# Preparing the keys of units 4 to 7 beside the first block inverse, and one list of VectorE background work

## The chip, the cores and the metric

The kernel runs on one core of one Trainium2 chip. Its metric is the device time of one execution in microseconds (us). The kernel before was timed three times: 815.86, 823.84 and 824.90 us, so the median is 823.84 us and the runs lie 1.1% apart.

## The reference

The work is a delta-rule linear attention (4 batches, 8 heads, 768 steps, head width 48), and then one dense block with a sigmoid-gated activation on the joined heads:

```python
k_n = k / (np.linalg.norm(k, axis=-1, keepdims=True) + 1e-06)
state = np.zeros((B, H, D, D))                    # B, H, S, D = 4, 8, 768, 48
for t in range(S):
    y[:, :, t] = einsum('bhd,bhde->bhe', q[:, :, t], state)
    v_old = einsum('bhde,bhd->bhe', state, k_n[:, :, t])
    state += beta[:, :, t, None, None] * einsum('bhd,bhe->bhde', k_n[:, :, t], v[:, :, t] - v_old)
x = y.transpose(0, 2, 1, 3).reshape(3072, 384)
h = x @ w_in                                      # w_in 384 x 2048
out = (h / (1 + exp(-1.702 * h))) @ w_out         # w_out 2048 x 384
```

The two weight matrices arrive as 64-bit floats. The kernel turns each pair of 32-bit words of a weight into one 32-bit float itself; q, k, v and beta are used as 32-bit floats.

## The kernel before, in words

**Units.** The sequence is cut into 6 chunks of 128 steps; with 4 batches that makes 24 units, numbered chunk by chunk (units 0 to 3 are chunk 0 of the four batches, units 4 to 7 chunk 1). For each unit the keys are normalised (`normalize...`), turned to `kT` on TensorE (`turn`, tile psT), and their Gram matrix `G` is formed (`gram`, tile psG). The recurrence inside a unit becomes a triangular solve in four blocks of 32 rows. The inverses of all 32x32 diagonal blocks of four units (later of two) are formed together on VectorE by `invert`, in the tiles NT (input, then result) and YB: one multiply by beta, 15 steps over the two 16x16 diagonal halves (`P<-NT,YB` and a reduce into YB), a copy on ScalarE of one half into NT (`NT<-YB 128x256`, called X1 below), then ten larger products that use this copy, and a last multiply by beta into NT (called the end of the inverse). The result goes through DRAM (Yd) into the tiles XB.

**Solving.** `hops(a, b)` solves two units side by side in eight hops. In each hop TensorE multiplies by the inverse (psU), ScalarE copies the result into US, TensorE forms what it takes from the lower blocks (psR), and VectorE subtracts that from V. `put_out` then forms the unit's outputs and state (psY) and writes them, transposed, into xT. `scores` turns the queries (psT, QS) and forms the masked scores (psQ, M).

**The dense block.** `hidden` multiplies xT of two units with w_in (tile ph) and applies the activation on ScalarE into gT; it is written as a generator of 16 slices of TensorE work. `both_written` and `written` multiply gT with w_out (tile po) for the first four units; from the third pair on, `seven` does it with seven half-size products instead of eight, for which `combined` has to form four sums and differences of w_out blocks on GpSimd (POOL), once.

**Order.** All queues are written by hand: nearly every instruction is pinned to program order on its engine, and a recording helper puts them all on one line of the source (L109 in the profile). The start runs: normalise and turn units 0 to 3; send the 32x32 diagonal blocks of their Gram matrices (psD, tile `TW`) through DRAM (Nd) into NT; `gram` 0 to 3; scores of units 0 to 3, with the first inverse beside them on VectorE; hops of units 0 and 1; hops of units 2 and 3 with the first slices of `hidden` between them; then the keys of units 4 to 7 (`keys`, `prepare`: normalise, turn, gram, `G` through DRAM into NT); the second inverse beside the rest of `hidden`; then the loop `woven` over units 3 to 24, which fills the solves with slices of the dense block from a queue.

**Weights.** `conversions` yields after each VectorE instruction, and `fill(n)` emits the next n of them. One piece of a weight takes five: mask the exponent (`ts`, followed by an activation on ScalarE), set the mantissa bits into a scratch in TW (`ts`), add the low word (`stt`), merge the sign (`stt`), multiply (`stt`). The raw words of w_in are kept in the w_out tile, two quarters at a time; finishing piece 1 and piece 3 of w_in issues the fetch of the next quarter on the SP queue.

**Padding work.** `warm(n)` issues n matmuls whose results are not used.

Of the kernel before, what the change touches and what calls it, by code (L numbers as in the profile page):

```python
# [18 lines left out]
def kernel(  # L19
# [179 lines left out]
    turns = [0]  # L199

    def conversion(dst, raw, shape):

        lo, hi = raw[:, :, :, 0], raw[:, :, :, 1]
        ts, stt = vec.tensor_scalar, vec.scalar_tensor_tensor
        AND, OR = ALU.bitwise_and, ALU.bitwise_or
        E1 = 1 << 20  # L210
        p = dst.bitcast(I32)
        ts(p, hi, 0x7FF * E1, None, op0=AND)
        act.activation(p, p, ACT.Relu, scale=8.0, bias=low)
        yield
        turns[0] ^= 1
        at = 3072 + turns[0] * 768
        t = TW[:, at : at + shape[0] * shape[1]].bitcast(I32).rearrange("p (j n) -> p j n", j=shape[0])
        f = t.bitcast(F32)
        ts(t, hi, E1 - 1, E1, op0=AND, op1=OR)
        yield  # L220
        stt(out=f, in0=lo.bitcast(U32), scalar=2.0**-32, in1=t, op0=ALU.mult, op1=ALU.add)
        yield
        stt(out=p, in0=hi, scalar=-(1 << 31), in1=p, op0=AND, op1=OR)
        yield
        stt(out=dst, in0=f, scalar=2.0**-20, in1=dst, op0=ALU.mult, op1=ALU.mult)
        yield
# [60 lines left out]
    converting = conversions()  # L287

    def fill(n):
        for _ in range(n):  # L290
            next(converting, None)

    ready = {}
    inverse = {}

# [53 lines left out]

    def transposed(src, dst):  # L350
        psT = ps_big.tile([128, NP, 128], F32, tag="big", name="psT")
        flat = src.rearrange("p h d -> p (h d)")
        for j in range(NP):
            pe.transpose(psT[:, j, :], flat[:, j * 128 : (j + 1) * 128], ident)
        act.activation(dst, psT, ACT.Copy)
# [24 lines left out]
    def turn(n):  # L380
        kTs[n] = wk.tile([128, NP, 128], F32, tag="kT", name="kT", bufs=5)
        transposed(KN[n % len(KN)], kTs[n])
# [28 lines left out]
    def diagonal(b, D_):  # L411

        kT = kTs[b]
        ps = [ps_seq.tile([128, NP, 128], F32, tag="seq", name="psD") for _ in range(2)]
        for h in range(H):
            r = slice(h % 2 * 64, h % 2 * 64 + D)
            pe.matmul(
                ps[h % 2][:, h // 2], lhsT=kT[r, h // 2, :], rhs=kT[r, h // 2, :],
                start=True, stop=True,
            )  # L420
        for e in range(2):
            for blk in range(NB):
                u = slice(blk * BS, (blk + 1) * BS)
                copy = vec.tensor_copy if e == 0 or blk == 0 else act.copy
                copy(D_[u, e::2, :], ps[e][u, :, u])
# [91 lines left out]
    class Step:  # L517
# [114 lines left out]
        def state(self, psS=None):  # L632
# [3 lines left out]
            for h in range(H):  # L636
# [4 lines left out]
                )  # L641
            St = ST[:, self.b, 0 : NP * D].rearrange("p (j d) -> p j d", j=NP)
            vec.tensor_tensor(St, psS, St, op=ALU.add)

        def outputs(self, state=False):
# [5 lines left out]
            if state:  # L651
                self.state(self.psS)
# [67 lines left out]
    def combined():  # L720

        for o, a, b in ((T1, W12, W11), (T2, W22, T1), (T3, W22, W12), (T4, W21, T2)):
            add(o, a, b, sub_)
# [160 lines left out]
    def follow(n):  # L884
# [8 lines left out]
        if n % HB == 0 and n > B:  # L893
            h = (n - 1) // HB
            gT, sums = [], []
            queue.append(hidden(xTs[h], gT, slice(0, NTH), 1.3, sums))
# [73 lines left out]
    for i in range(B, len(KN)):  # L970
        pool.memset(KN[i][:, :, D:DP], 0.0)

# [13 lines left out]
    for b in range(B):  # L986
# [3 lines left out]
        )  # L990
    for b in range(B):
        load(b, ((QP, q),), sync)
    for b in range(B):
        load_values(b, sync)
    fetch_in(1, other_queue)
    for n in range(B, len(KN)):
        load(n, ((KN, k),), sync)
# [3 lines left out]
    for b in range(B):  # L1001
        gram(b)
        warm(NA)
    late_U = spare("U")[:, 0 : H * D + XR]
    pair = [new_step(n) for n in range(B)]
    inverting = invert(0)
    for n in range(B):
# [4 lines left out]
        if n == 0:  # L1012
            ahead_of(inverting, 18)
    run(inverting)
    pool.memset(late_U[:, H * D :], 0.0)
    for s in pair:
        s.select()
    fill(5)
# [9 lines left out]
    def put_out(s):  # L1028
        s.queries()
        s.outputs(True)  # L1030
        steps.pop(s.n)

    def keys():

        def unit(n):
            yield from normalize_mixed(n)
            yield from prepare(n)

        work = [unit(n) for n in range(B, 2 * B)]
        for t in range(18):  # L1040
            for u in range(B):
                s = t - 3 * u
                if s >= 0 and s % 2 == 0:
                    next(work[u], None)
            yield
        for w in work:
            run(w)

    path = hops(*pair[:2])
    for i in range(2 * NB):  # L1050
        together(*next(path))
        warm(NU)
        fill(1)
    for s in pair[:2]:
        put_out(s)
        fill(1)
    load(7, ((KN, k),), sync)
# [16 lines left out]
    preparing = keys()  # L1074
    for i in range(2 * NB):
        together(*next(path))
        if i > 2:
            feed()
        fill(2)
        ahead_of(preparing, 2 if i else 0)  # L1080
    for s in pair[2:]:
        put_out(s)
        feed()
        fill(2)
        ahead_of(preparing, 2)
# [4 lines left out]
    while not ("in", 7) in done:  # L1090
        fill(1)
    run(preparing)
    inverting = invert(1)
    first = new_step(B)
    for i in range(25):
        ahead_of(inverting, 1)
# [5 lines left out]
    run(inverting)  # L1102
    while ffn:
        feed()
    fill(10)
    def last_written():
        yield from written(*units[HB], gTs[1])
        combined()

    queue = [both_written(0, gTs[0]), last_written()]  # L1110
# [34 lines left out]
```

## Time and profile before

| what | value |
|---|---|
| runs | 815.86, 823.84, 824.90 us (median 823.84) |
| profiled execution | span 813.5 us from the first to the last instruction; the page gives no other time of it, and the three runs are 2.4 to 11.4 us longer than this span |
| TensorE busy | 748.9 us, 92% of the span; mean granted clock 0.943 |
| VectorE, ScalarE, GpSimd busy | 501.4, 238.5 and 249.4 us |
| weight-load side of TensorE | 636.4 us |
| DMA | 54.45 MB, mean 67 GB/s |
| chain that ended last | PE 70%, DVE 16%, DMA 4%, POOL 3% |

In the profile PE is TensorE, DVE is VectorE, ACT is ScalarE, POOL is GpSimd and SP the engine that issues most DMAs. A timeline line gives the start and the duration in us, the engine, the line, the operation, output and input tile with partitions x elements, and how many instructions were merged; in brackets stands the idle time before it and what ended that. In a table by stage each engine has its busy time and its instructions, then come the granted TensorE clock (1 is full speed) and the share of the DMA engines.

### The profile page before, as it was taken

The page shows a single profiled execution, that of the slowest core. Times are in us where ns is not written, and L with a number is a line of the kernel's source. Part 1 is how long each engine was busy: PE and PEld are TensorE (multiplying, and loading weights), DVE is VectorE, ACT ScalarE, POOL GpSimd, SP SyncE. Part 2 cuts the span into 40 slices and gives each one's busy share as a digit, 9 for nine tenths or more (in the row PEclk, how much of TensorE's full clock was granted, in tenths as well). Part 3 has the DMA queues.
Part 4 walks back from the last instruction along what each step waited for, and adds up shares of the span by engine and source line. Part 5 has one row for each costly group of instructions (what it writes and reads, how often), then busy time and mean ns, then how long its engine had stood idle before and what let it go on. Part 6 is the DMA issues. An engine that isn't in the chain of part 4 may idle for free.

```text
span 813.5 us, 19675 instructions
## 1 busy us (share of the span) xinstructions
PE 748.9 (92%) x8464; PEld 636.4 (78%) x8464; DVE 501.4 (62%) x1029; ACT 238.5 (29%) x523; POOL 249.4 (31%) x210
## 2 busy tenths in 40 slices
PE   8678889777789779999999999999999999999998
PEld 6566668644456669889888898898898898998988
DVE  5797581998578667668767777786676681110000
ACT  3332263223323322242232232332422312312120
POOL 5011030011023826235254262282160330502213
PEclk9576599889799989999999999999999999999999
DMA  9945466244112410420421323224204102000000
GB/s 163 148 74 106 102 173 163 43 111 118 55 50 66 102 45 18 103 63 18 106 53 42 83 54 74 58 56 103 56 18 94 21 15 47 2 25 2 22 3 19
DMA packets 143654, 54.45 MB, mean 67 GB/s; under 512 B 113664, under 2 KB 138368, under 8 KB 143568
## 3 DMA queue, kind: packets, MB, share of 16 engines
q1 hardware_dynamic: 141936, 48.42, 27.0%
q0 software_dynamic: 1536, 4.52, 2.3%
q8 instruction: 66, 1.08, 0.6%
q10 hardware_dynamic: 96, 0.26, 0.1%
q14 instruction: 20, 0.16, 0.1%
HBM read 33.13 MB, written 18.87 MB: 64 GB/s over the span
## 4 chain that ended last, share of the span: by engine, by line
PE 70%; DVE 16%; DMA 4%; POOL 3%; issue 3%; SPq 2%; ACT 1%; DVEq 0%; POOLq 0%
PE ph L109 25%; PE po L109 24%; PE psY L109 6%; PE psU L109 5%; DVE P L109 4%; PE psQ L109 3%; DVE YB L109 3%; PE psT L109 2%; DVE TW L109 2%; PE psG L109 2%; SPq L109 2%; PE psR L109 2%; DVE NT L109 2%; DVE w_out L109 2%; POOL TW L711 1%
## 5 line engine op out<-in xcount | busy, mean ns | idle before, releaser
L109 PE MATMUL ph<-xT,w_in 128*128 128x256 f32 x1152 | 268.7, 390 | 0.0
L109 PEld LDWEIGHTS ph<-xT,w_in 128*128 128x128 f32 x1152 | 219.8, 194 | 33.3 <-DVE V L109 1.4
L109 PE MATMUL po<-w_out,gT 128*128 128x192 f32 (+1 forms) x736 | 152.8, 361 | 18.7 <-DVE w_out L109 11.0
L109 PEld LDWEIGHTS po<-w_out,gT 128*128 128x128 f32 x736 | 122.3, 193 | 37.2 <-DVE w_out L109 14.8
L711 POOL TENSOR_TENSOR gT<-gT 128x512 f32<-128x512 f32 x80 | 105.8, 1331 | 124.6 <-ACT gT L109 114.1
L109 DVE TENSOR_TENSOR V<-V,psR 64x384 f32<-64x384 f32 (+1 forms) x96 | 53.3, 556 | 134.7 <-PE psR L109 133.5
L109 DVE TENSOR_TENSOR P<-NT,YB 64x2 f32<-64x2 f32 (+9 forms) x200 | 98.4, 492 | 6.4
L109 ACT ACTIVATE gT<-ph 128x512 f32<-128x512 f32 x92 | 54.9, 596 | 152.9 <-PE ph L109 152.8
L109 PEld LDWEIGHTS psU<-V,XB 32*32 32x32 f32 x1536 | 61.6, 109 | 31.5 <-issue 16.5
L109 DVE TENSOR_REDUCE YB<-P 64x2 f32<-64x2 f32 (+9 forms) x200 | 81.8, 409 | 6.9
L109 PE MATMUL po<-TW,gT 128*128 128x192 f32 x480 | 83.0, 328 | 0.0
L109 ACT COPY US<-psU 32x384 f32<-32x384 f32 x92 | 43.2, 469 | 125.0 <-PE psR L109 115.4
L109 PE MATMUL psU<-V,XB 32*32 32x48 f32 x1536 | 73.0, 209 | 6.5 <-DVE V L109 4.8
L109 PEld LDWEIGHTS po<-TW,gT 128*128 128x128 f32 x480 | 77.9, 190 | 1.1 <-issue 0.3
L109 PE MATMUL psR<-US,G 32*32 32x48 f32 x2208 | 63.1, 207 | 0.6 <-ACT US L109 0.5
L578 POOL TENSOR_SCALAR_AFFINE_SELECT M<-M 128x1024 f32<-128x1024 f32 x19 | 23.6, 1245 | 123.5 <-DVE M L109 62.1
L109 DVE TENSOR_TENSOR o<-o,po 128x192 f32<-128x192 f32 x40 | 13.5, 351 | 75.8 <-PE po L109 75.3
L109 PEld LDWEIGHTS psR<-US,G 32*32 32x32 f32 x2208 | 53.5, 108 | 2.0 <-ACT US L109 1.1
L94 POOL DMA_DIRECT2D KN<-in_k_dram x15 | 14.4, 959 | 99.0 <-PE psY L109 99.0
L109 DVE TENSOR_TENSOR P<-NT 64x512 f32<-64x512 f32 (+7 forms) x50 | 43.0, 860 | 2.1
L109 PE MATMUL ps_warm<-ident 128*128 128x256 bf16 x176 | 31.5, 339 | 11.4 <-ACT G L109 6.5
L109 PE MATMUL psQ<-QS,kT 48*128 48x176 f32 (+1 forms) x368 | 35.5, 337 | 4.9 <-ACT QS L109 4.8
(110 smaller groups left out, 776.8 us busy)
## 6 DMA issues: line engine op xcount, KB each, us to landing
Nd<-G SPq DMA_DIRECT2D x20, 512.0 KB, 3.5
V<-in_v_dram SPq DMA_DIRECT2D x24, 192.0 KB, 3.2
out_dram<-o SPq DMA_DIRECT2D x24, 192.0 KB, 2.6
QP<-in_q_dram SPq DMA_DIRECT2D x22, 192.0 KB, 3.4
w_out<-in_moe_w_in_dram SPq DMA_DIRECT2D x18, 192.0 KB, 4.6
raw<-in_moe_w_out_dram SPq DMA_DIRECT2D x9, 384.0 KB, 4.0
NT<-Nd SPq DMA_DIRECT2D x24, 128.0 KB, 2.6
XB<-Yd SPq DMA_DIRECT2D x24, 128.0 KB, 3.1
```

Of the source, the lines that this page charges most:

```text
L94: dma(out=place(dst, n)[:, :, 0:D], in_=src[b, :, c * C : (c + 1) * C, :].rearrange("h p d -> p h d"),)
L109: return lambda *a, **kw: tc.keep_in_program_order(op(*a, **kw))
L578: (pool if self.n < B else nc.gpsimd).affine_select(out=self.M, in_=self.M, compare_op=ALU.is_gt, fill=0.0, base=0, pattern=[[0, H], [1, 1 ...
L711: (engine or nc.gpsimd).tensor_tensor(o, a, b, op=op)
```

## The change

Four things are changed.

1. The keys of units 4 to 7 are loaded early (into three KN tiles and a fourth place KX in TW), normalised by `normalize_second` between steps of the first inverse, and turned and multiplied to diagonal blocks behind the scores of units 0 to 3; the blocks are copied out by ScalarE alone (`shared=False`) and sent from the ScalarE queue. `keys` and `prepare` are no longer used for these four units; their `gram` calls move into the hops, two of them in place of a `warm`.
2. `fill` draws from one list, `background`: conversion of w_in, then the second inverse, then conversion of w_out. The number of instructions that each place draws is changed.
3. A conversion keeps its intermediate values in the raw words themselves, at every second 32-bit word, and the order of the five instructions is changed.
4. `combined` is cut into 16 slices, which are drawn beside the 16 slices of the third `hidden`, and no longer follow `written` in one go.

```diff
 def conversion(dst, raw, shape):
     ts(p, hi, 0x7FF * E1, None, op0=AND)
     act.activation(p, p, ACT.Relu, scale=8.0, bias=low)
     yield
-    turns[0] ^= 1
-    at = 3072 + turns[0] * 768
-    t = TW[:, at : at + shape[0] * shape[1]]...
-    ts(t, hi, E1 - 1, E1, op0=AND, op1=OR)
+    stt(out=p, in0=hi, scalar=-(1 << 31), in1=p, op0=AND, op1=OR)
     yield
-    stt(out=f, in0=lo.bitcast(U32), scalar=2.0**-32, in1=t, op0=ALU.mult, op1=ALU.add)
+    ts(hi, hi, E1 - 1, E1, op0=AND, op1=OR)
     yield
-    stt(out=p, in0=hi, scalar=-(1 << 31), in1=p, op0=AND, op1=OR)
+    f = lo.bitcast(F32)
+    stt(out=f, in0=lo.bitcast(U32), scalar=2.0**-32, in1=hi, op0=ALU.mult, op1=ALU.add)
     yield
     stt(out=dst, in0=f, scalar=2.0**-20, in1=dst, op0=ALU.mult, op1=ALU.mult)
...
+def background():
+    converting = conversions()
+    while ("in", 7) not in done:
+        next(converting)
+        yield
+    yield from invert(1)
+    done.add("inverse")
+    yield from converting
...
+def normalize_second():
+    z, r = (...)
+    for o in range(0, B, 2):
+        for i in range(2):
+            act.activation(sq[:, i], home(B + o + i)[:, :, 0:D], ACT.Square)
+        yield
+        vec.tensor_reduce(z[:, o : o + 2], sq, axis=AX.X, op=ALU.add)
+    for o in range(B):
+        pool.tensor_tensor(r[:, o], z[:, o], half, op=ALU.pow)
+    yield
+    vec.tensor_scalar(r, r, 1e-6, None, op0=ALU.add)
+    vec.reciprocal(r, r)
+    for o in range(B):
+        K = home(B + o)[:, :, 0:D]
+        vec.tensor_tensor(K, K, r[:, o].broadcast_to([128, H, D]), op=ALU.mult)
+    yield
...
 def combined():
+    n = 2
     for o, a, b in ((T1, W12, W11), (T2, W22, T1), (T3, W22, W12), (T4, W21, T2)):
-        add(o, a, b, sub_)
+        for f in range(0, HF, n):
+            add(o[:, f : f + n], a[:, f : f + n], b[:, f : f + n], sub_)
+            yield
...
-    for b in range(B):
-        gram(b)
-        warm(NA)
+    scaling = normalize_second()
+    inverting = invert(0)
+    gram(0); warm(NA); gram(1); warm(NA)
+    next(scaling)
+    gram(2); warm(NA); gram(3); warm(NA)
+    ahead_of(inverting, 9)
+    next(scaling)
+    ahead_of(inverting, 4)
+    next(scaling)
+    ahead_of(inverting, 2)
+    run(scaling)
...
     for n in range(B):
         next(pair[n].scored)
         warm(NA)
         run(pair[n].scored)
         warm(NA)
-        if n == 0:
-            ahead_of(inverting, 18)
+        turn(B + n)
+        diagonal(B + n, Dx[:, n], False)
+        Nd = dram.tile([H * C * BS], F32, tag="Nd", name="Nd", bufs=4)
+        beside(out=Nd.rearrange("(h p k) -> p h k", p=C, k=BS), in_=Dx[:, n])
     run(inverting)
+    for b in range(B):
+        sync(out=NT[...], in_=Ndx[b]...)
...
-    fill(5)
+    fill(7)
...
 # hops of units 0 and 1
     together(*next(path))
-    warm(NU)
-    fill(1)
+    if i in (2, 5):
+        gram(B + i // 3)
+    else:
+        warm(NU)
+    fill(2)
...
-    load(7, ((KN, k),), sync)
+    sync(out=KN[0], in_=KX)
...
 # hops of units 2 and 3
     together(*next(path))
+    if i in (2, 5):
+        gram(B + 2 + i // 3)
     if i > 2:
         feed()
     fill(2)
-    ahead_of(preparing, 2 if i else 0)
...
-while not ("in", 7) in done:
-    fill(1)
-run(preparing)
-inverting = invert(1)
 for i in range(25):
-    ahead_of(inverting, 1)
+    fill(1)
     feed()
```

## The prediction

> **What bounds the kernel now.** I read the busy slices first.
>
> ```profile
> ## 2 busy tenths in 40 slices
> PE   8678889777789779999999999999999999999998
> ...
> PEclk9576599889799989999999999999999999999999
> ```
>
> From the fifteenth slice (304 us) on TensorE is full at full clock: the tables by stage give it 502.1 of 509.5 us. Nothing in this change can shorten that. Before 304 us it has 246.8 us of busy time, so 57 us idle, and many of the busy ones at half clock. The stages:
>
> ```profile
> 20.00:58.40 38.40, 27.18 (x204) 21.65 (x205) 33.26 (x69) 15.81 (x38) 0.00 (x0) 0.64 0.71 104
> 58.40:81.30 22.90, 20.34 (x376) 14.66 (x373) 18.23 (x22) 6.02 (x11) 6.02 (x6) 0.65 0.55 117
> ...
> 89.00:125.40 36.40, 30.25 (x409) 23.81 (x410) 25.11 (x44) 17.78 (x34) 9.77 (x7) 0.77 0.69 167
> 125.40:142.50 17.10, 17.10 (x91) 14.79 (x91) 1.17 (x2) 4.67 (x8) 0.15 (x1) 1.00 0.62 164
> 142.50:172.00 29.50, 22.42 (x99) 18.63 (x97) 27.63 (x59) 6.54 (x14) 1.09 (x1) 0.88 0.16 29
> ```
>
> The columns are PE, PEld, DVE, ACT, POOL, clock, DMA. Read DVE (third): 1.17 of 17.1 us while the keys of units 4 to 7 go through DRAM, then 27.6 of 29.5 in the second inverse. Behind it come the stalls that end on this inverse, on w_out, and on POOL. The waits from 125 to 305 us and POOL's timeline:
>
> ```profile
> DVE NT L109 <- DMA NT<-Nd: 20.5, 2, 15.9
> PE psT L109 <- POOL KN L309: 12.8, 3, 7.9
> PE po L109 <- DVE w_out L109: 11.0, 7, 2.9
> ```
>
> ```profile
> 267.27 3.44 POOL L711 TENSOR_TENSOR TW<-w_out 128x1536 f32<-128x1536 f32 x1
> 270.79 3.43 POOL L711 TENSOR_TENSOR w_out<-w_out 128x1536 f32<-128x1536 f32 x1
> 274.17 7.81 POOL L711 TENSOR_TENSOR TW<-w_out,TW 128x1536 f32<-128x1536 f32 x2
> ```
>
> The change aims at all of these. What it pays shows in ScalarE's timeline of the first inverse:
>
> ```profile
> 43.73 0.65 ACT L109 COPY M<-psQ 128x256 f32<-128x256 f32 x2 [0.21 <-PE psQ L109]
> 44.27 0.66 ACT L109 ACTIVATE NT<-YB 128x256 f32<-128x256 f32 x1
> 45.35 0.60 ACT L109 ACTIVATE QS<-psT 128x512 f32<-128x512 f32 x1 [0.43 <-PE psT L109]
> ```
>
> The second is X1. The inverse's products from 50.08 us on read it, and it stands behind one unit's scores. In the changed code it is emitted by `run(inverting)`, behind the scores, turn and diagonal blocks of all four units.
>
> **Step 1, the first inverse (end A, before 58.4 us).** VectorE gets two reduces of 128x768 (0.95 each, as the inverse's own), a scale and a reciprocal (0.53) and four key multiplies (0.49 each), and waits: the second pair of squares on ScalarE stands behind the last G copy (39.73), so its reduce ends at 41.8; two of the four POOL powers (1.65 each, by the rn rows) follow, to 45.2. Step 15 starts at 47.7 instead of 41.59, key 4 is ready at 46.3, and the steps up to X1's readers take 8.5 us, to 56.2. Up to there DVE's work hides ScalarE's.
>
> ScalarE and TensorE now pass each unit back and forth. At half clock: QS 0.60; from its end to the end of psT of the new key 3.79 (psQ 2.0, warm 0.6, psT 1.06, as at 40 to 45 us; the M copies lie inside); kT 0.60; psD 2.1; eight copies of 32x128 on ScalarE at 0.26, 2.1; issue of Nd 0.42: 9.7 with gaps. At full clock psQ, psT and psD are 1.16, 0.60 and 1.16, and it is 7.3. Unit 4 ends at 46.3+6.5=52.8, unit 7 29 us later at 81.9; X1 82.6; the rest of the inverse as before 8.3 (50.08 to 58.40): A=91. At full clock 83. The row that decides: from 28 to 40 us the tables show a clock of 0.50 with TensorE busy 9.3 of 12 us (78%); the new loop is busy 7.5 of 9.7 (77%). I take A=90, 32 us later than now.
>
> The Trainium skill (TensorE: Matmul & The Clock Gate, section "What's actually happening") says that one busy window of about 3.4 us opens the clock; the loop has stretches of 3.7 us, so by the page A would be near 83, and the sum below 7 us lower. The row at 40 to 47.6 us, with 7.6 us of unbroken work before the clock rose, speaks against it.
>
> On the queues: SP's four key loads (0.57 each, 2.3) move ahead of the query loads, the second quarter of w_in and V. QP, issued at 27.1 now and 3.4 us on its way, still lands before its use at 39.9 (9 us of cover); the others are used after A. The third quarter's fetch waits behind four short NT loads (0.34 each). POOL's four powers stand where it had nothing to do from 12.3 to 58.5. The four Nd writes leave SP, where G went out at 0.37 each, for ScalarE, where QS stands behind them.
>
> **Step 2, A to the end of the fourth unit's outputs (B, now 125.4, that is A+67).** Nine conversion instructions stand ahead of the first V subtraction instead of six, under POOL's four selects, which stretch them (1.57 for 0.94): it comes at A+10.3, not A+7.8. Each hop then has two conversions of 0.96 beside its subtraction (0.56, 1.14 in two hops): 2.5 us, against 2.4 now, where TensorE's hop and its four warm matmuls (1.45+1.03) are the bound. Two grams at half clock (2.08 for a warm's 1.03) add 2. The fetch of the last quarter, issued at A+19 and 8.5 to 10.4 us on its way (63.57 to 72, 91.53 to 101.96), is waited for about 1.5 us; ST and the xT copies stand behind it. The third unit's first subtraction comes at A+37 (now A+30.75): +6.2. Then the normalisation is gone: no powers in VectorE's way at 111 to 118 and no 5 us wait for the fetch at 97. Five hops with hidden's slices (1.5 each at full clock, 2.9 at half), two grams and two outputs take 28 us: B=A+65=155.
>
> **Step 3, hidden and the second inverse.** The inverse starts in the fourth hop of that pair and has ten of its steps done by B; what is left took 150.12 to 171.2, so it ends at A+84=174 (now 171.2). TensorE has 25 slices of 1.3, psT and psQ left: B+34.5, C=189.5. Now the last ph ends at 169.4 and the inverse at 171.2, so that w_out arrives late; then the conversions have 15 us of lead.
>
> **Step 4, w_out and combined.** From 173.5 to 267.2 TensorE is idle 16.1 us, 11.0 of it on w_out. With the lead these go, and some 4.5 us that the half clock cost in 200 to 220: 93.7-11-4.5+1=79. So the third hidden starts at 268.5 (now 267.2). There the sixteen slices of 384 cost POOL 0.87 each (ksq and KN rows of that size: 0.82 to 1.03), 13.9 in all for 14.7, but a key multiply waits for one or two and not for four: the wait of 7.9 becomes 2 to 3, as at 236 and 257 us, and the half clock behind it (18 ph in 5.65, elsewhere 3.9) goes: -6.5.
>
> Sum: +1.3-6.5=-5.2, span 808.3. The profiled span 813.5 lies 10.3 below the median 823.84; I put the difference on the median: **818.5 us**.
>
> Unknown: a write to every second word is in no row. Contiguous it is 0.96 for 768; the dearest such row beside POOL is 1.73; no gain is likely as the operation reads strided already. I take 0.96.
>
> **The rivals.** *The loop runs at full clock, or ScalarE gets through it sooner.* A=83, everything after keeps its distance: 811.5. For it: the clock stayed at 1.0 from 47.6 to 56 even with 1.6 of 4 us busy. Against: it first has to rise.
>
> *The in-place writes are dear.* If a strided write costs double, 0.96 more, 14 of them lie in the hops, where VectorE is already the bound (2.5 us a hop): +13.4; 28 on w_out at about 0.55 take 15 us, all of C's lead, and bring back some 5 of the 11 us: 837. From 0.9 us extra an instruction on it is slower by over 1%. For it: every read of hi and lo is strided and two-operand forms of 768 already take 0.95, where w_out's take 0.55. Against: reading that way costs 0.95, not 1.9.
>
> *The new lead buys nothing.* If w_out still stalls TensorE because its fetches, not VectorE, are late, the 11 us stay: 829.5, still within 1%. Against: the waits name DVE.
>
> **How the numbers follow.** About 1% (8 us) is what a measurement of this kernel tells from no change. The forecast, including the third rival, has 0.42 and its own range 815 to 830; the full clock or quicker loop, with other gains that bring it under 815.6, 0.38; dear writes or other losses above 832, 0.20. Faster 0.38, same 0.42, slower 0.20. The range for 8 in 10 reaches to 800 (A=83, and 11 us less idle time in the hops) and 836.
>
> **What would show it.** In the profile after: NT<-YB of the first inverse at 75 to 83 us and VectorE idle some 20 us before it; YS end at 83 to 91; the second inverse's first multiply between 125 and 145 with no wait on Nd; po waits for w_out under 3 us; POOL slices of 0.87; no wait of psT over 4 us. An X1 at 60 us, or hops of 3.5 us, would make it wrong.

## The result and the profile after

The changed kernel takes 829.35 us in the median of four runs, the kernel before 820.94 in the median of four, which is 1.0102 of it. The ratio used from here on compares fast runs with fast runs alone and is 1.0122 (95% interval 1.0078 to 1.0166). The changed kernel is slower by some 1%, where the forecast had 818.5 us, a gain. The profiled execution of after (828.2 us of span) stands near its kernel's median, that of before (813.5) below the fastest of its four; so the 14.7 us between the two profiles overstate the difference (8 to 10 us) by some 5.

The stages of after, cut at the forecast's own landmarks. Columns: PE, PEld, DVE, ACT, POOL busy, granted clock, DMA share, GB/s.

```profile
20.00:58.40 38.40, 23.86 (x181) 18.72 (x182) 30.18 (x68) 17.64 (x44) 6.72 (x4) 0.65 0.75 116
58.40:91.10 32.70, 16.08 (x119) 12.69 (x118) 8.00 (x13) 12.29 (x39) 0.00 (x0) 0.60 0.08 13
91.10:126.00 34.90, 25.77 (x434) 20.62 (x434) 27.15 (x34) 10.65 (x18) 6.97 (x6) 0.60 0.64 138
126.00:161.40 35.40, 32.12 (x491) 26.28 (x490) 21.39 (x48) 13.19 (x29) 2.48 (x3) 0.70 0.42 123
161.40:196.30 34.90, 34.90 (x174) 30.45 (x173) 26.33 (x47) 10.70 (x22) 1.48 (x2) 1.00 0.45 93
196.30:289.50 93.20, 79.94 (x930) 51.12 (x928) 72.36 (x150) 30.50 (x67) 31.31 (x26) 0.91 0.26 71
289.50:323.70 34.20, 31.00 (x346) 26.21 (x344) 20.75 (x48) 11.31 (x25) 17.65 (x17) 0.95 0.35 79
323.70:828.20 504.50, 497.18 (x5734) 446.37 (x5732) 279.24 (x584) 135.09 (x304) 176.65 (x134) 1.00 0.20 46
```

Read the second row against the others: for 32.7 us VectorE works 8 and TensorE 16. The last row is the same in every kernel of this study, 504.4 or 504.5 us from the first product of the seven to the end. All that follows happens before it. As differences to before, in us:

| landmark | before | after | change forecast | change measured |
|---|---|---|---|---|
| A, end of the first inverse | 58.4 | 91.1 | +31.6 | +32.7 |
| B, end of the fourth unit's outputs | 125.4 | 161.4 | +29.6 | +36.0 |
| C, last ph of the first two hiddens | 169.4 | 196.3 | +20.1 | +26.9 |
| D, first ph of the third hidden | 268.6 | 289.5 | +1.3 | +20.9 |
| E, first product of the seven | 309.0 | 323.7 | -5.2 | +14.7 |

So the price (A) came as forecast, and the repayment did not: between A and E 36.8 us were to come back, and 18.0 did (some 23 if the difference of the times, and not of the two profiles, is taken). The rows behind the price, ScalarE's and then VectorE's timeline of after:

```profile
76.65 0.60 ACT L109 ACTIVATE kT<-psT 128x512 f32<-128x512 f32 x1 [0.54 <-PE psT L109]
79.41 2.13 ACT L109 COPY TW<-psD 32x128 f32<-32x128 f32 x8 [2.16 <-PE psD L109]
81.57 0.37 ACTq L109 DMA_DIRECT2D Nd<-TW  x1
82.11 0.64 ACT L109 ACTIVATE NT<-YB 128x256 f32<-128x256 f32 x1 [0.57 <-ACT TW L109]
```

```profile
82.78 0.43 DVE L109 TENSOR_TENSOR P<-NT 128x256 f32<-128x256 f32 x1 [24.66 <-ACT NT L109]
```

X1 (NT<-YB) stands behind the eight psD copies of the fourth unit, and VectorE waits 24.66 us for it.

Then the repayment. VectorE's rows in which it waits for a fetch or for TensorE, with its other work queued behind them:

```profile
110.50 0.69 DVE L109 TENSOR_SCALAR w_in<-w_out 128x768 int32<-128x768 int32 x1 [4.44 <-DMA w_out<-in_moe_w_in_dram]
...
124.04 0.69 DVE L109 TENSOR_SCALAR w_in<-w_out 128x768 int32<-128x768 int32 x1 [0.81 <-DMA w_out<-in_moe_w_in_dram]
...
139.77 0.36 DVE L109 TENSOR_SCALAR w_out<-raw 128x384 int32<-128x384 int32 x1 [3.89 <-DMA raw<-in_moe_w_out_dram]
...
187.80 0.42 DVE L109 TENSOR_TENSOR V<-V,psQ 128x96 f32<-128x96 f32 x2 [5.37 <-PE psQ L109]
...
197.50 0.56 DVE L109 SCALAR_TENSOR_TENSOR w_out<-w_out 128x384 int32<-128x384 int32 x1 [2.83 <-ACT w_out L109]
```

TensorE's waits of after from C to D, and then from D to E, each with total, number, longest:

```profile
PE psT L109 <- POOL KN L320: 7.8, 3, 3.0
PE po L109 <- DVE w_out L109: 5.4, 4, 2.0
```

```profile
PE psT L109 <- POOL KN L320: 3.2, 1, 3.2
```

The keys' wait between D and E, 7.9 in before, is now 3.2: this is what the slices were forecast to do. GpSimd's slices:

```profile
290.72 1.00 POOL L743 TENSOR_TENSOR w_out<-w_out 128x384 f32<-128x384 f32 x1
291.68 5.81 POOL L743 TENSOR_TENSOR TW<-w_out,TW 128x384 f32<-128x384 f32 x5
```

1.0 us each (forecast 0.87), so sixteen cost 16 us instead of 14.7, and still the stage is 6.2 us shorter.

### The profile page after: what moved, and what is told of

Same layout as the page of the kernel before. It is cut to its first block, busy times and chain, and to the rows that moved or that the text cites. A ratio compares the mean times of both kernels' runs of the same rounds, so it can differ in the third digit from the quotient of the medians.

```text
span 828.2 us, 19822 instructions
## 1 busy us (share of the span) xinstructions
PE 757.2 (91%) x8520; PEld 645.3 (78%) x8520; DVE 495.0 (60%) x1021; ACT 246.8 (30%) x555; POOL 254.4 (31%) x223
## 4 chain that ended last, share of the span: by engine, by line
PE 73%; DVE 8%; issue 6%; DMA 5%; POOL 4%; ACT 2%; SPq 1%; ACTq 0%; DVEq 0%; POOLq 0%
PE ph L109 29%; PE po L109 22%; PE psY L109 5%; PE psU L109 5%; PE psQ L109 4%; PE psT L109 3%; PE psR L109 2%; PE psG L109 2%; DMA w_out<-in_moe_w_in_dram 2%; PE psD L109 1%; DVE w_out L109 1%; DMA xT<-last 1%; SPq L109 1%; DVE P L109 1%; DVE w_in L109 1%
## 5 line engine op out<-in xcount | busy, mean ns | idle before, releaser
L109 PE MATMUL ph<-xT,w_in 128*128 128x256 f32 x1152 | 265.4, 387 | 0.0
L109 PE MATMUL po<-w_out,gT 128*128 128x192 f32 (+1 forms) x736 | 148.8, 355 | 9.1 <-DVE w_out L109 5.4
L109 PEld LDWEIGHTS psU<-V,XB 32*32 32x32 f32 x1536 | 63.6, 112 | 36.8 <-issue 17.3
L109 PE MATMUL psU<-V,XB 32*32 32x48 f32 x1536 | 75.1, 212 | 10.6 <-DVE V L109 9.1
L109 PE MATMUL psR<-US,G 32*32 32x48 f32 x2208 | 65.5, 212 | 1.6 <-ACT US L109 1.6
L109 DVE TENSOR_TENSOR P<-NT 64x512 f32<-64x512 f32 (+7 forms) x50 | 44.0, 880 | 26.6 <-ACT NT L109 24.7
L109 PEld LDWEIGHTS psR<-US,G 32*32 32x32 f32 x2208 | 55.7, 112 | 3.0 <-ACT US L109 1.9
L109 PEld LDWEIGHTS <-ident 128*128 128x128 bf16 x168 | 18.9, 118 | 27.2 <-issue 20.1
```

Source lines behind the costliest of these rows:

```text
L109: return lambda *a, **kw: tc.keep_in_program_order(op(*a, **kw))
```

## The experiments

The theory: the change is dear because of the order in which the four units' loop is emitted, behind which X1 stands, and it is repaid too little because a lead in time is no lead where VectorE's queue is written out in order. The rivals: what is saved ahead of the hops is lost again behind them; the losses are TensorE's clock or VectorE's capacity; a part that was held harmless (in-place writes, slices) costs. Ratios are to the kernel before, run on the same chip, with 95% intervals; the changed kernel has 1.0122 [1.0078, 1.0166].

### The price: where X1 stands, and how the loop is ordered

**X1 early** (e1):

```
         turn(B + n)
+        if n == 0:
+            ahead_of(inverting, 3)
         diagonal(B + n, Dx[:, n], False)
```

> One line is added to the changed kernel: after the first unit's scores and the turn of unit 4's key, three steps of the first inverse are emitted, so that ScalarE's X1 copy (NT<-YB) stands behind one unit of the loop and no longer behind four. Theory 'late X1': the copy ends at 48 to 55 us instead of 82.8, VectorE's wait of 24.7 us for it goes, and the first inverse ends at 66 to 72 instead of 91. TensorE still has the loop of four units to finish (79.4 us in the changed kernel), so hop 0 can start at 83 to 86 instead of 95.6: 10 to 12 us of the span come back, time against the kernel before 0.996 to 1.001 (the changed kernel has 1.0122). Rival 're-lost': what is won before the hops is lost again to fetches that VectorE's queue then waits for in the hops (the fetch of the last quarter of w_in and the first rows of w_out are issued at fixed places of the program and take 8 to 10 us each): under 4 us come back, 1.007 or more. Rival 'the loop itself': ScalarE's and TensorE's exchange is what sets hop 0; then the wait goes and hop 0 stays above 90 us.

**Loop split and X1 early** (e2):

```
         run(pair[n].scored)
         warm(NA)
-        turn(B + n)
-        diagonal(B + n, Dx[:, n], False)
+        if n == 1:
+            ahead_of(inverting, 3)
+    turn(B)
+    for n in range(B):
+        if n + 1 < B:
+            turn(B + n + 1)
+        diagonal(B + n, Dx[:, n], False)
```

> In the changed kernel the loop over the four units is split: the scores of all four units first, with X1 behind the second of them, and then the turn of each new key, with the diagonal blocks of a unit emitted behind the turn of the next one, so that TensorE need not wait for each kT copy. Theory 'late X1 and the exchange': loop ends at 66 to 72 us (79.4 before), the first inverse at 64 to 70, hop 0 at 71 to 77 instead of 95.6: 18 to 24 us come back, time against the kernel before 0.983 to 0.991. Rival 're-lost downstream': under 8 us come back, 1.002 or more. Rival 'the loop itself', in which the exchange is bound by ScalarE's busy time and not by the order of emission: loop end above 76 us, and 0.996 to 1.001, as with X1 moved alone.

**Loop split, X1 late** (e5): the same without the two lines of X1.

> The changed kernel with the loop split as in the second run (scores of all four units, then turns and diagonal blocks), but X1 left where it was, emitted behind the loop. With the two runs before it this makes a square: loop split or not, X1 early or late. If the order of the loop and the place of X1 each cost by themselves: loop end at 70 us as with both, X1 at 71 to 74, first inverse's end A at 79 to 83, hop 0 at 84 to 88 (96.1 in the changed kernel, 80.2 with X1 early alone, 75.1 with both): 8 to 12 us come back, time against the kernel before 0.997 to 1.003. Rival 'X1 alone is the cost' (the split of the second run only helped as it let X1 through): hop 0 stays above 92 us and the time above 1.007.

Measured:

| | X1 late | X1 early |
|---|---|---|
| loop as changed | A 91.1, hop 0 at 96.1; 1.0122 | A 73.0, hop 0 at 80.2; 1.0027 [0.9996, 1.0057] |
| loop split | A 75.0, hop 0 at 79.6; 0.9952 [0.9914, 0.9990] | A 69.2, hop 0 at 75.1; 0.9883 [0.9843, 0.9923] |

Both matter, the split more: 1.7% by itself (more than was expected), X1 0.95%, both 2.4%. The split alone makes the change faster than the kernel before, on all else unchanged; "X1 alone is the cost" falls. The split holds two reorderings, the scores first and each unit's diagonal blocks behind the next turn; no run tells them apart. Why the split works shows in TensorE's timeline, after first, the split loop (e5) second:

```profile
69.70 1.16 PE L109 MATMUL psD<-kT 48*128 48x128 f32 x16 [0.69 <-ACT kT L109]
70.79 0.66 PE L109 MATMUL psT<-ident,TW 128*128 128x128 f32 x4
71.29 0.49 PE L109 MATMUL ps_warm<-ident 128*128 128x256 bf16 x3
74.17 1.16 PE L109 MATMUL psQ<-TW,kT 48*128 48x128 f32 x16 [2.39 <-ACT TW L109]
```

```profile
46.33 0.50 PE L109 MATMUL ps_warm<-ident 128*128 128x256 bf16 x3
46.66 0.60 PE L109 MATMUL psT<-ident,TW 128*128 128x128 f32 x4
47.10 0.49 PE L109 MATMUL ps_warm<-ident 128*128 128x256 bf16 x3
47.95 1.16 PE L109 MATMUL psQ<-QS,kT 48*128 48x128 f32 x16 [0.36 <-ACT QS L109]
```

In the changed loop the next unit's queries are turned, and then TensorE waits 2.39 us until ScalarE has copied the eight diagonal blocks that stand ahead of their QS copy (TW here). With the scores together the wait in e5 is 0.36 us. Over its whole loop, 41.5 to 63.0 us, TensorE is busy 17.2 of 21.5 us at a granted clock of 0.90, and in e2, 45.8 to 70.0 us, 18.6 of 24.2 at 0.85; in the changed loop, 43 to 79.4 us, it is busy 25.4 of 36.4 and has 0.64. The loop of e5 ends at 63.0 us instead of 79.4.

**X1 early alone** shows the rival at work, too. Hop 0 came 15.8 us sooner, more than expected, and 7.8 us are left of it (1.0027 for 1.0122): from A to the fourth unit's outputs it took 80.1 us for 69.3 in after (both to the end of the last psY). VectorE waited 8.94 us for the third quarter of w_in. SP's queue in that run says why:

```profile
73.04 0.80 SPq L109 DMA_DIRECT2D Yd<-NT  x2
75.03 9.85 SPq L109 DMA_DIRECT2D XB<-Yd  x4
84.94 1.96 SPq L109 DMA_DIRECT2D NT<-Nd  x4
87.00 21.72 SPq L109 DMA_DIRECT2D w_out<-in_moe_w_in_dram  x24
```

The XB loads wait for the two Yd writes that are issued from ScalarE's queue, behind the loop's copies (9.85 us here, 2.41 in after), and the fetch stands behind them.

### A to B: the fetches in VectorE's queue

**Conversion steps inside the loop** (e6):

```
         run(pair[n].scored)
         warm(NA)
+        if n < 3:
+            fill(2)
         turn(B + n)
...
-    fill(7)
+    fill(1)
```

> The changed kernel with six of the seven conversion steps that stand behind the first inverse emitted in the loop of the four units, two behind the scores of each of the first three. VectorE has nothing to do there (it waits 24.7 us for X1), and the fetch of w_in's third quarter, which stands behind one of these steps, goes out at about 60 us instead of 98. Theory 'A to B was missed by the fetches that VectorE's queue waits for': the wait of 4.4 us for w_in in the first hops goes, the first V subtractions come some 5 us sooner, and from the first inverse's end to the fourth unit's outputs it takes 62 to 67 us instead of 70.3; one more copy in ScalarE's loop costs 0.7 to 1.5 us: time against the kernel before 1.003 to 1.008 (changed kernel 1.0122). Rival 'TensorE at half clock bounds the hops': that stretch stays at 69 to 71 us, 1.010 to 1.016.

1.0028 [0.9996, 1.0059]: 0.94% below the changed kernel, a little more than expected. From A to the last psY it took 60.0 us for 69.3. The fetches of the third and of the last quarter of w_in in e6:

```profile
55.41 10.98 SPq L109 DMA_DIRECT2D w_out<-in_moe_w_in_dram  x12
...
103.70 6.72 SPq L109 DMA_DIRECT2D w_out<-in_moe_w_in_dram  x12
```

The first goes out at 55.41 instead of 98.14, and the wait of 4.44 us is gone. The edit does two things, and VectorE's rows tell them apart: the first V subtraction came at A+7.7 instead of A+10.1, as six steps fewer stand ahead of it, and the first one behind the fetch (V<-V,psR 64x384) at A+13.2 instead of A+20.1. The rival, hops bound by TensorE whatever VectorE does, falls. How the 9.3 us divide on TensorE is less clear. Its rows from A to the last psY, in after, in e6, and in e4, which has the program of after up to there:

```profile
91.10:160.40 69.30, 56.88 (x917) 46.00 (x915) 47.66 (x78) 23.30 (x45) 8.80 (x8) 0.64 0.54 132
88.00:148.00 60.00, 50.71 (x917) 40.31 (x914) 41.11 (x71) 22.39 (x44) 7.27 (x8) 0.77 0.47 126
93.70:160.60 66.90, 53.42 (x917) 42.54 (x914) 47.67 (x77) 23.30 (x45) 8.80 (x8) 0.72 0.54 137
```

Against after, 3.1 of the 9.3 us are idle time (9.3 for 12.4), and 6.2 are the same 917 matmuls at a granted clock of 0.77 instead of 0.64. But e4, e7, e10, e11 and e15, all with the program of after in this stretch, have clocks of 0.64 to 0.72 and 66.9 to 70.6 us. So part of the 6.2 us is what one execution differs from another, and that the shorter gaps brought the clock up is not shown.

### C to D: what the lead on w_out is worth

**Scores of unit 4 later** (e4: slices 22 and 24) and **earlier** (e7: 2 and 4):

```
-        if i == 16:                   # e4: 22, e7: 2
             next(first.scored)
-        if i == 18:                   # e4: 24, e7: 4
             run(first.scored)
```

> In the changed kernel the scores of unit 4 are emitted at slices 22 and 24 of the first two hiddens instead of 16 and 18, nothing else. Between the end of the second inverse (180.8 us) and 188 VectorE stood 5.4 us before V<-psQ, with w_out's conversions behind it. Theory 'that stop costs the w_out lead': the stop goes or shrinks under 2 us, TensorE's waits for w_out (5.4 us) fall by 3 or more, and the span loses 3 to 6 us: 1.005 to 1.009 against the kernel before (1.0122 for the changed one). Rival 'the lead is worth nothing there': the waits move to another place and the span changes by under 2 us, 1.010 to 1.015. Rival 'later is worse': the unit's scores then come too late for the weave and the span grows by 2 us or more.

> The opposite of the fourth run: the scores of unit 4 are emitted at slices 2 and 4 of the first two hiddens instead of 16 and 18, nothing else. VectorE leads TensorE the more the further the slices go (its inverse ends while TensorE is at slice 16), so its stop before V<-psQ (5.4 us at 18, 8.1 us at 24) should shrink to under 2 us at 4. Theory 'the stop costs the w_out lead': TensorE's waits for w_out (5.4 us in all) fall to 0 to 3, the time from the last ph of the first two hiddens to the third hidden's first falls from 93 to 87 to 91, and the time is 1.004 to 1.010 of the kernel before. Rival 'the conversions' own length and ScalarE's share of them set the waits': these stay at 4 to 6 us and the time at 1.010 to 1.015.

Later: 1.0249 [1.0202, 1.0295], the rival "later is worse", and my expectation missed: VectorE's stop before V<-psQ grew to 8.11 us. VectorE runs ahead of TensorE here, so a later place waits longer. Earlier: the stop fell to 2.92 us, and nothing that can be measured came of it. The time was 1.0105 [1.0066, 1.0143] (changed kernel 1.0122). C to D took 90.4 us, but so it did in e1, e5 and e6 (90.1 to 90.5), where the scores stand as in the changed kernel; the 93.2 of after belongs to that execution. TensorE's waits in the profile of e7:

```profile
PE psT L109 <- POOL KN L320: 8.4, 3, 3.0
PE po L109 <- DVE w_out L109: 5.4, 4, 2.0
```

The second line, 5.4 us in 4 places, is the same to the last digit in the profiles of after, e1, e2, e5, e6, e7 and e8. So is a row of VectorE that stands 1.1 to 1.2 us behind C in each of these: in after at 197.50 with C at 196.3, shown above, in e7 at 196.05 with C at 194.9. It waits 2.8 us for ScalarE, whose timeline of after shows what for:

```profile
196.37 0.60 ACT L109 ACTIVATE TW<-ph 128x512 f32<-128x512 f32 x1 [1.99 <-PE ph L109]
196.86 0.61 ACT L109 ACTIVATE w_out<-w_out,low 128x384 int32<-128x384 int32 x1
```

The conversion's step on ScalarE stands in its queue behind the activation of the hidden's last slice. However early VectorE is, it restarts here just behind C, and what follows is the same. (e7's earlier scores also ended the second inverse 2.8 us later. VectorE's time for w_out between that and C is 11.3 us in e7; in after it is 15.5 less the stop of 5.4, so little over 1 us was won.)

**w_out hardly converted** (e9): four of five VectorE instructions and ScalarE's of each w_out piece are left out.

```
         ts(p, hi, 0x7FF * E1, None, op0=AND)
+        if short:                     # pieces of w_out
+            for _ in range(5):
+                yield
+            return
```

> The changed kernel with each w_out piece converted by its first VectorE instruction alone; the other four, and ScalarE's one, are left out (w_out then holds masked words, so the two layers' numbers are others; every matmul, transfer and combination stays). This asks what a perfect w_out lead is worth between the last ph of the first two hiddens and the third hidden's first (93 us, forecast 79). Theory 'the conversions are the whole loss': TensorE's waits for w_out (5.4 us) and for keys (7.8) go, the clock stays up, and it takes 76 to 82 us: 0.995 to 1.001 of the kernel before. Rival 'another order is behind it': the waits for w_out go, the keys' waits behind GpSimd stay, and it takes 85 to 89 us: 1.002 to 1.008.

**30 steps ahead of the recurrence instead of 10** (e10):

```
-    fill(10)
+    fill(30)
     queue = [both_written(0, gTs[0]), written(*units[HB], gTs[1])]
```

> One number of the changed kernel is another: 30 conversion steps instead of 10 are emitted behind the second inverse, before the layer's products are woven into the recurrence; further on a piece is emitted only just before the product that reads it. In every profile so far TensorE's waits for w_out in that stretch were 5.4 us in 4 places, however early the stage before had ended. Theory 'the lead is a place in VectorE's queue, not a time': with four pieces more ahead of the recurrence's subtractions the waits fall under 1.5 us, the stretch from 93 to 86 to 89 us, the time to 1.004 to 1.009 of the kernel before. Rival 'VectorE's capacity' (72 of 93 us busy, without a gap from 198 to 213 us): the conversions now stand ahead of V subtractions, which come later by the same; psU waits for V, the stretch stays at 90 to 95 us, 1.010 to 1.018.

e9: 0.9997 [0.9969, 1.0025], and C to D 80.8 us for 93.2 (90.1 to 90.5 in e1, e5 and e6), as the first theory said: no wait for w_out left, TensorE busy 74.6 us at clock 0.96 instead of 79.9 at 0.91. The keys' waits, which that theory let go too, mostly stayed (6.2 us). So the forecast's 79 us is nearly there, but only without the conversions.

e10: the waits for w_out fell to 1.1 us, as expected from "a place in the queue", and the time rose to 1.0235 [1.0196, 1.0274]. The rival had the direction and the wrong victim. Not V was late but the keys; TensorE's and VectorE's rows:

```profile
216.42 1.11 PE L109 MATMUL psT<-ident,KN 128*128 128x128 f32 x4 [12.72 <-POOL KN L320]
```

```profile
209.98 0.54 DVE L109 TENSOR_REDUCE ssq<-ksq 128x8 f32<-128x384 f32 x1
```

The reduce that the next key's normalisation needs stands behind the 20 added steps: it came 15.4 us behind C (194.6), in after 3.6 (199.90 behind 196.3). In the queue as written, a step moved ahead for w_out is a step behind for something else.

**Two steps for each slice from slice 8 on** (e15, on top of e7), so that ScalarE's steps stand ahead of the last activations:

```
     for i in range(25):
-        fill(1)
+        fill(1 if i < 8 else 2)
```

> The run with unit 4's scores at slices 2 and 4 (1.0105, C to D 90.4 us), and from slice 8 of the first two hiddens on two steps of VectorE's list are emitted for each slice instead of one. So the conversions' steps on ScalarE stand ahead of the activations of the last slices and no longer behind them. Theory 'ScalarE's queue cuts the lead off': VectorE's two waits of 2.8 us for ScalarE ahead of C go or come down under 1, some ten steps more are done by then, TensorE's waits for w_out fall from 5.4 to 1 to 3.5 us without a longer wait for keys (8.4), and C to D takes 84 to 88 us: 1.002 to 1.008 of the kernel before. Rival 'only a place in VectorE's queue', as in run 10: the steps go ahead of the next keys' reduce again, the keys' waits rise by as much, C to D 89 to 96 us: 1.009 to 1.020.

C to D took 84.3 us (90.4 in e7) and no wait for w_out is left, as expected from ScalarE's queue; TensorE's waits for keys are 9.1 us. But the time is 1.0152 [1.0110, 1.0194], and from the last psY of the fourth unit to D it took 126.1 us, in e7 126.3. ScalarE's timeline of e15 shows where the gain went:

```profile
189.71 0.61 ACT L109 ACTIVATE w_out<-w_out,low 128x384 int32<-128x384 int32 x1 [7.35 <-DVE w_out L109]
190.23 1.06 ACT L109 ACTIVATE gT<-ph 128x512 f32<-128x512 f32 x2
```

The conversion's step now waits 7.35 us for VectorE, which is still at the inverse (its end is at 188.5), and the hidden's activations stand behind it; TensorE's ph waits 3.96 us for that. The stall is ahead of C instead of behind it. With the conversions as they are, five orders (after, e4, e7, e10, e15) gave 126 to 137 us from the fourth unit's outputs to D; without them (e9) it is 116.8.

### The parts alone

**Slices in the kernel before** (e3), and **the changed kernel without them** (e11):

```
-            add(o, a, b, sub_)
+            for f in range(0, HF, n):
+                add(o[:, f : f + n], a[:, f : f + n], b[:, f : f + n], sub_)
+                yield
```

> The kernel before with one part of the change alone: the four w_out combinations are cut into 16 slices of 128x384, one emitted beside each slice of the third hidden. If the slicing is the whole gain that the changed kernel shows between the third hidden's first ph and the first product of seven (34.2 us for 40.4), the wait of psT for KN of 7.9 us falls to about 3 and the span loses 5 to 7 us: 0.991 to 0.994 of the kernel before. Rival 'the gain belongs to the other parts' (the keys of units 4 to 7 no longer crowd POOL there): the interval stays at 39 to 41 us and the time within 2 us, 0.998 to 1.002.

> The changed kernel with the w_out combinations whole again, four instructions behind the third layer's last product, as in the kernel before. The third run showed the third hidden's stretch at 34.3 us with the slices alone, but the time within 0.5% of the kernel before. If the slices are worth what that stretch shows, it goes from 34.2 to 39 to 41 us here and the time to 1.016 to 1.022 of the kernel before. Rival 'in the changed order GpSimd's work fits anyway': the stretch stays at 34 to 36 us, 1.010 to 1.014.

The stage D to E answers alike from both sides: 34.3 us with slices in the kernel before (40.4 without), 40.1 without them in the changed one (34.2 with). TensorE's longest wait there, e3 first, then e11:

```profile
PE psT L109 <- POOL KN L309: 2.7, 1, 2.7
```

```profile
PE psT L109 <- POOL KN L320: 8.7, 1, 8.7
```

The whole time answers less: 0.9981 [0.9933, 1.0029] for e3 and 1.0147 [1.0101, 1.0194] for e11. Each is a difference of some 2 us (e3 to the kernel before, e11 to the changed one) with 4 to 5 of uncertainty, where the stage shows 6. That the stage is shortened is shown; how much of it the time keeps is not.

**In-place conversion in the kernel before** (e12): the five instructions of a conversion in the order of the change, with its writes into the raw words.

> The kernel before with one part of the change alone: the conversion's fourth instruction writes its masked word in place and the sign goes in before it. From the changed kernel's rows the in-place form of 128x768 costs 0.69 us where the separate one cost 0.92 to 0.95: 14 in the hops and 28 shorter ones on w_out save at most 0.25 and 0.2 each. Theory 'no part of the loss': 0.994 to 1.001 of the kernel before. Rival 'in-place writes make the next instruction wait' (the reader of hi stands right behind its writer): 1.005 or more.

1.0009 [0.9970, 1.0047]: no part of the loss, and no gain that can be measured. The in-place instruction takes 0.694 us against 0.945 for the one that wrote to a scratch.

### Putting it together

**All three edits** (e8), **with 8 warm-ups instead of 28 ahead of hop 0** (e13), **with X1 late** (e14). The first is e2 plus e6 plus e7; e13 changes NY from 28 to 8 in it; e14 leaves the X1 lines of e8 out, and e16 is e13 with the two steps of e15.

> The second run's split loop with X1 early, and the two edits of runs six and seven on top: conversion steps inside the loop, scores of unit 4 at slices 2 and 4. If the three gains add: hop 0 at 71 to 77 us, 5 us less up to the fourth unit's outputs, 2 to 5 less behind it: 0.974 to 0.984 of the kernel before (the split alone gave 0.988). Rival 'they overlap': in the split loop VectorE idles less, so the conversions delay the first inverse and only half of it comes: 0.984 to 0.989.

> The run with all three edits, with 8 warm-up matmuls ahead of hop 0 instead of 28. Theory 'the warm-ups in TensorE's queue set hop 0 there': hop 0 starts 4 to 5.5 us behind the first inverse's end instead of 8.4, and the time goes from 0.983 to 0.976 to 0.980 of the kernel before. Rival 'the warm-ups pay for themselves': the hops run longer at half clock, from hop 0 to the fourth unit's outputs 59 us or more instead of 56.7, and the time is 0.982 to 0.990.

> The run with all three edits, but X1 left behind the loop, so that VectorE has a gap that the conversions fill (10.2 us of it with the split alone). Theory 'the conversions delay the steps ahead of X1's readers': they cost nothing here, first inverse's end at 75 to 79, hop 0 at 80 to 83, time as with all three: 0.980 to 0.987. Rival 'X1 early is worth its 0.7% here too' (split alone 0.995, with X1 early 0.988): 0.988 to 0.994.

> The fastest kernel so far (split loop, X1 early, conversion steps inside the loop, early scores, 8 warm-ups; 0.9804) with the same two steps for each slice. Theory 'ScalarE's queue cuts the lead off': 3 to 6 us less, 0.973 to 0.978 of the kernel before. Rival: 0.979 to 0.990.

e8 has 0.9829 [0.9779, 0.9880], at the upper end of what was expected for a sum; against the split loop's 0.9883 [0.9843, 0.9923] that is 0.5%, where e6 and e7 had gained 1.1% together, and the intervals overlap. In its profile (808.0 us, its median is 801.5) hop 0 stood right behind the 28 warm-ups:

```profile
76.26 5.46 PE L109 MATMUL ps_warm<-ident 128*128 128x256 bf16 x28
81.66 0.52 PE L109 MATMUL psU<-V,XB 32*32 32x48 f32 x8
```

e13: 0.9804 [0.9756, 0.9852], the fastest kernel of the study (800.41 us, before 817.57) and faster than both kernels; whether it is faster than e8 can't be told. Hop 0 came 6.3 us behind A instead of 8.3, then waiting for XB, and the hops took 58.5 us instead of 56.7 at a clock of 0.61 for 0.70. In these two profiles both theories hold in part and cancel. e14: 0.9932 [0.9899, 0.9966], the rival: X1 early is worth about 1% here too. The conversions in VectorE's gap do not make up for a late X1. e16: 0.9871 [0.9831, 0.9910], no gain over e13, as in e15.

## Why the prediction was wrong, point by point

**Step 1, the price, held.** A was to come 31.6 us later and came 32.7 later, X1 at 82.1 for 82.6. The row that decided between the clocks (busy 78% at half clock) was the nearer one: the loop had 0.64, busy 70%. The Trainium skill (TensorE: Matmul & The Clock Gate, section "What's actually happening") lets one busy window of about 3.4 us open the clock, which by the working's estimate would have made A 83; A was 91.1, though the clock did open for part of the loop (0.85 from 66.8 to 73.6 us). Seven profiles with the same program up to A (after, e4, e7, e9, e10, e11, e15) have it between 89.3 and 94.7.

**Step 2 failed on "waited for about 1.5 us".** The first V subtraction came at A+10.1, as forecast (A+10.3). But the steps that I moved ahead of the hops moved the queue past its fetches. Measured were 4.44 and 0.81 us for w_in and 3.89 for w_out, which was not in the sum at all: 9.1 for 1.5 (8.9 to 10.2 in e4, e7, e10, e11 and e15). A to B took 70.3 for 65. e6 removes the largest of these waits, takes six steps from behind A, and brings 9.3 us in its profile; how much of this is the wait's, how much the clock's, stays open.

**Step 3 held.** B to C took 34.9 us for 34.5. The lead that I counted on, second inverse's end to C, was 15.5 us for 15. That it fits so well is partly luck: B=155 and the 21.1 us from 150.12 to 171.2 give 176 for the inverse's end and not 174, and so a lead of 13.4; what was left at B took 19.4 us.

**Step 4 failed on "with the lead these go, and some 4.5 us that the half clock cost".** It is the largest miss: C to D changed by -6.0 us in the two profiles, forecast -18.8. The stretch in before, a wait in it that the forecast does not show, and the stretch in e5, which has the program of after there:

```profile
169.40:268.60 99.20, 79.17 (x928) 50.09 (x928) 79.17 (x167) 31.63 (x69) 22.46 (x18) 0.93 0.34 86
PE po L109 <- ACT w_out L109: 4.1, 1, 4.1
180.20:270.50 90.30, 76.51 (x929) 48.51 (x927) 72.36 (x150) 30.39 (x67) 30.87 (x26) 0.94 0.27 73
```

The profiles add it up. The waits for w_out, 15.1 us in before (11.0 on VectorE, 4.1 on ScalarE's step ahead of the first po), fell to 5.4, not to nothing (5.4 missing). (The 4.1 us were let go without a word, as the sum starts at 173.5 for before and at C for after.) TensorE's busy time was to fall by 4.5: in after it stayed, 79.9 for 79.2 (5.3 missing), but in e1, e5 and e6 it was 76.3 to 76.9 and C to D 90.1 to 90.5, so that some 2.6 of the 4.5 came in those executions, at a clock of 0.94, and the change is near -9 there. The keys' waits rose from 5.0 to 7.8, where 1 was allowed (1.8 missing). The mistake is one of reading: the profile before names VectorE as the releaser of these waits, and I took this to mean that time for VectorE would cure them. VectorE got 15.5 us of lead and could use only part of them: it stood 5.37 us for unit 4's scores and 2.83 for its own step on ScalarE, which stands behind the hidden's last activation. e10 and e15 put the conversions further ahead and moved the stall to the keys and to the hidden's activations; e9 shows that some 10 us more are there when the conversions are taken away, and no order that was run has them. Whether some other order of these queues keeps part of them stays open.

**The slices held.** D to E changed by -6.2 us, forecast -6.5. (The 267.2 that the working calls the third hidden's start in before is the psQ just ahead of its first ph, which starts at 268.6; as the working goes by the psQ on both sides, its +1.3 stands.)

**The rivals.** "The in-place writes are dear" fell (e12). "The loop runs at full clock" fell for the kernel as changed; where the loop is split (e5) the clock was 0.90 in it, and A came at 75.0. "The new lead buys nothing" was given 829.5 us, and measured were 829.35, which is luck: the waits for w_out did fall, from 15.1 to 5.4 us, what was left of them did not name late fetches, and another 5 us were lost in step 2, which this rival leaves alone. It was right in that a lead for VectorE is not yet a gain, and I dismissed it with "the waits name DVE".

**The direction.** The forecast let a large, sure loss be repaid by a long list of gains, each read from a stall. The loss came at once and whole. Of the gains, those of step 3 and of the slices came whole; those of steps 2 and 4, behind queues that are written out in order, came in part or not at all.

## What to carry to other kernels

Before work is moved, look for what will stand in front of it on each engine: here one 0.64 us copy, emitted behind a loop that another engine paces, cost VectorE 24.7 us, and reordering that loop, with the copy moved forward, won back twice what the whole change had lost (2.4% for 1.2%). A stall "released by VectorE" is only cured by an earlier VectorE if the instruction can move up in its queue; ask what stands ahead of it and what it would push back. And when a price is certain and its repayment is a sum of cured stalls, check for each gain that the queue lets it through.

## What the hardware showed beyond that

The granted clock differs from execution to execution, and with it the length of equal work: the 917 matmuls from A to the fourth unit's outputs took 56.9 us at 0.64 in after and 53.4 at 0.72 in e4, with the same program, and 50.7 at 0.77 in e6. It also moves equal code about. e8 and e13 have the same program up to the warm-ups, and the loop ended at 76.3 in the one profile and 72.3 in the other; in e2 and e5 the first QS copy, with the same instructions ahead, stood at 45.8 and 41.5 us, with a clock of 0.50 and 0.64 from 20 to 41 us. The skill's section named above says that the activity window runs free of the program, which would make such a spread; no run here shows the window itself. A landmark of one profile is thus known to some 5 us before the stage at full clock (A above: 89.3 to 94.7).

Writing every second word in place was cheaper than writing the scratch in one piece. VectorE's groups of 128x768 in the hops of before and after:

```profile
L109 DVE TENSOR_SCALAR TW<-w_out 128x768 int32<-128x768 int32 x5 | 4.7, 945 | 0.0
```

```profile
L109 DVE TENSOR_SCALAR w_out<-w_out 128x768 int32<-128x768 int32 x7 | 4.8, 693 | 0.2
```

Busy us and mean ns stand behind the bar: 945 and 693 ns for the same operation on the same words. Why is open; the layout of the output and the tile both differ. It is not the strided write as such: the mask of 128x768 that before writes in one piece into w_in takes 0.69 us too (at 69.52 us), and for 128x384 nothing is gained (351 ns into the scratch in before, 362 in place in e12).
